# Seven-product second layer: halves of one expert's F instead of pairs of experts

## The chip, the cores and the metric

The kernel runs on one core of one Trainium2 chip. The metric is the time of one execution on the device, in microseconds (us). Engines are named as in the profile: PE (TensorE matmuls), PEld (its weight loads), DVE (VectorE), ACT (ScalarE), POOL (GpSimd), SP (SyncE, which issues most DMAs).

## The reference

Two stages, one after the other. The first is a gated linear attention over 4 sequences (batches) of 768 steps, 8 heads of 48: a state of 48 x 48 per head is decayed by a sigmoid gate, gets k v added, and is read with q. The second is a layer of four experts on the 3072 tokens of width 384:

```python
for t in range(S):
    state = f[:, :, t, :, None] * state + np.einsum('bhd,bhe->bhde', k[:, :, t], v[:, :, t])
    y[:, :, t] = np.einsum('bhd,bhde->bhe', q[:, :, t], state)
...
p = domain_probs / (domain_probs.sum(-1, keepdims=True) + 1e-09)
for e in range(E):                       # E = 4, w1[e]: 384 x 1024, w2[e]: 1024 x 384
    h = np.maximum(x @ w1[e], 0.0)
    out += p[:, e:e + 1] * (h @ w2[e])
```

All inputs and the output are float32; the kernel's matmuls work on bfloat16.

## The kernel before

**Work.** Time is cut into six chunks (c = 0 to 5) of 128 steps. One chunk has 4 x 128 = 512 tokens, four blocks of 128, one for each batch (b, or nt in the second layer). For each chunk the attention is computed first: loads of f, k, q, v; gates and their logarithms on ACT; cumulative sums on PE (`cs`, in chunk 0 also `cq`); exponentials; the products of q and k with them (`q c.b`, `k c.b`, line 385 or 388, on DVE or POOL); transposes (`tp`); scores (`at`), their masked eviction (`ev_at`); the output `y`; the state update. The result, transposed, is the input x of the expert layer.

**Expert layer.** The first product is h = relu(x w1[e]); F = 1024 is eight slices of 128 (`h c.e.fc.n0`, line 489, and `hs` for the later groups, line 521), evicted with relu on ACT or DVE. The second product is done in two ways.

- *Plain* (`mm_o`, line 504): chunk 0 (four blocks) and the first half of chunk 1 (two blocks), all four experts. For each block and expert eight matmuls with 384 moving columns, and one eviction of 128x384 that multiplies by the token's probability and adds to o (`ev_o`, line 511).
- *Seven products* (`mm_p`, line 558): from chunk 1's second half on, in groups of (chunk, half of the batches, pair of experts), named `c.hf.p`. The probabilities are put on y before, so that a pair of experts is one matrix product: rows are two blocks of 128 tokens, the inner side is the two experts of the pair, the output is two halves of 192 columns. Strassen's scheme in Winograd's form computes these 2 x 2 x 2 blocks with seven products instead of eight. It needs four sums of h blocks for each group (`s_sum`, line 539, 128x1024, on DVE, tiles S), and four differences of w2 blocks once for each pair (`t_sum`, line 548, 128x1536, on DVE; three go to `ts_sb`, the fourth replaces a part of w2 itself, so it must come after the pair's last plain product). Each product is eight matmuls of 192 columns into one PSUM bank; the bank is evicted into o (`ev_p`, line 566; 128x192), in the order 1, 2, 6, 5, 7, 3, 4. Banks X (1, 6, 7, 4) and Y (5, 3) go on accumulating after an eviction, so a later product of a bank waits for the eviction of the one before. The very last group, called TAIL (5.1.1), has the order 1, 2, 5, 6, 4, 7, 3 and stores some rows in halves.

**Order.** Everything is put into a list of `Op`s with a name, planned durations for the engines that can run it, a priority, dependences and buffers that it takes and frees ("rooms": 8 PSUM banks, 3 h, 6 S, 3 o tiles, and so on). `Plan.run` is a list scheduler: whenever an engine is free in the plan, it takes the ready step of lowest priority number. The instructions are then emitted in the planned order, and each engine's queue runs them in that order; what a step really waits for is a semaphore. `MOVES` is a string of named offsets on priorities, some with a fixed engine (`@DVE`). The priority of the expert layer is a counter, `unit`, that grows by one for each step of the layer. `zip_units` lays h of one expert beside the second product of the expert before; `zip_groups` does so for groups. DMA loads of the weights and of v are issued by POOL in the order `SEQ` (`v0 v1 v2 w0 v3 w1`, then the other pieces); the first two v wait for a k load to have landed (`GATE`). All other loads, the DMA transposes and the stores are issued by SP.

Of the kernel before, what the change touches and what calls it, by code (L numbers as in the profile page):

```python
# [9 lines left out]
BF16 = mybir.dt.bfloat16  # L10
# [5 lines left out]
    "ld f0.0=-58.8;ld f0.1=-61.7;ld k0.1=-53.8;ld f0.2=-42.3;ld k0.2=-2.1;ld v0.0=1520.4;w 0=-1521;ld v0.3=-2.1;w 5=-34.9;"  # L16
    "gate1 0.2=-7.8;cs 0.0=-2.4;expq 0.1=40.3;cs 0.1=-2.2;exps 0.1=-7;q 0.2=-0.1@DVE;ev_tp 0.3=196.8;ev_at0 0.0=17.1;ev_at1 0.0=13.1;"
    "ev_y 0.0=5.6;ev_at0 0.1=201.7;kv 0.0=-185.8;ld p=23.8;ev_tp 1.1=11.6@DVE;ev_y 1.1=-9.1;ev_ys 1.2.0.0=31.4@ACT;ev_ys 1.2.0.1=0@ACT;"
    "ld v2.2=16.8;h 0.0.4.0=27.1;h 0.0.4.128=38.5;h 0.0.4.256=24.1;o 0.2.0.1=1.7;h 0.3.2.0=11;h 0.3.4.0=12.2;h 0.3.6.0=-9.4;"
    "ev_o 0.2.3.0=-24;q 2.2=37;ev_at1 2.1=-11.4;xs 2.1.0=-40.5;ev_at0 2.2=26;xs 2.3.1=-2.9;ld f3.0=-13.6;ld q3.0=-1;ld f3.2=-3;"  # L20
    "ld v3.2=1.8;store 0.1.0=6.7;store 0.3.0=28.6;o 1.1.1.0=9;h 1.2.5.0=49.9;h 1.3.0.0=5.4;o 1.2.0.0=38.3;h 1.3.1.0=10;h 1.3.3.0=14.6;"
    "relu 1.3.6.0=7.5@ACT;t 1.1=-34;store 1.0.0=-1;o 1.3.1.0=-14.9;store 1.1.0=13.4;s2 1.1.0=-42.2;relu_s 1.1.1.0.0=5.1@DVE;"
    "ev_p 1.1.0.1=-44.4@DVE;p 1.1.0.2=-3.1;ev_p 1.1.0.2=-5.1;relu_s 1.1.1.0.2=5.9;p 1.1.0.6=7.9;p 1.1.0.5=3.9;ev_p 1.1.0.5=-49.4@DVE;"
    "relu_s 1.1.1.1.4=-0.1;relu_s 1.1.1.0.6=-2.9@DVE;egs 3.1=-4.1;v 3.1=4.7;tp 3.1=-27.9;tp 3.2=7.5;xs 3.1.0=-33.4;"
    "ev_ys 3.1.1.0=-36.5@DVE;ev_at0 3.3=-38.8;ev_kv 3.0=41.7;sf 3.0.3=21.3;kv 3.3=7.5;ld q4.0=-17.9;ld k4.2=18.2;ld q4.2=4.1;"
    "hs 2.0.0.1.2=-1.1;relu_s 2.0.0.1.4=67.6;hs 2.0.0.1.6=-7.8;hs 2.0.1.0.0=3;hs 2.0.1.1.2=-11.2;hs 2.0.1.1.4=-6.5;hs 2.0.1.1.6=3.3;"
    "hs 2.1.0.1.2=-6.2;ev_p 2.0.1.7=-10.7;hs 2.1.0.0.6=-11.8;hs 2.1.0.1.6=-7.5;s1 2.1.0=-35;p 2.1.0.1=3.8;p 2.1.0.2=22.9;"
# [110 lines left out]
def kernel(  # L138
# [11 lines left out]
    nc = tc.nc  # L150
# [27 lines left out]
    DH = Din // 2  # L178
    P = Plan(rooms)
# [48 lines left out]
    ts_sb = wpool.tile([128, NPR, 3, KF, DH], BF16)  # L228
# [273 lines left out]
    def mm_o(c, e, nt, fcs, part, cols):  # L502
        for fc in fcs:
            nc.tensor.matmul(out=tl("op", c, e, nt, part)[:, cols], lhsT=tl("h", c, e, half_of(c, nt * T))[:, fc, nt * T:(nt + 1) * T],  # L504
                             rhs=w2_sb[:, e, fc, cols], start=(fc == 0), stop=(fc == KF - 1))

    def ev_o(c, e, nt, part, cols, eng):
        op, o = tl("op", c, e, nt, part)[:, cols], tl("o", c, nt // 2)[:, nt % 2, cols]
        pe = pn[:, e, nt * C + c:nt * C + c + 1]
        if e > 0:  # L510
            nc.vector.scalar_tensor_tensor(out=o, in0=op, scalar=pe, in1=o, op0=ALU.mult, op1=ALU.add)
        elif eng == "ACT":
            nc.scalar.activation(out=o, in_=op, func=AF.Copy, scale=pe)
        else:
            nc.vector.tensor_single_scalar(out=o, in_=op, scalar=pe, op=ALU.mult)
# [15 lines left out]
    def block(c, hf, p, r, el):  # L531
        return tl("hs", c, hf, p)[:, el, :, r * T:(r + 1) * T]

    def s_sum(c, hf, p, j, fs):
        a = lambda r, el: block(c, hf, p, r, el)[:, fs]
        s = lambda i: tl("S", c, hf, p, i)[:, fs]
        in0, in1, op = {1: (lambda: (a(1, 0), a(1, 1), ALU.add)), 2: (lambda: (s(1), a(0, 0), ALU.subtract)),
                        3: (lambda: (a(0, 0), a(1, 0), ALU.subtract)), 4: (lambda: (a(0, 1), s(2), ALU.subtract))}[j]()
        return nc.vector.tensor_tensor(out=s(j), in0=in0, in1=in1, op=op)  # L539
# [3 lines left out]
    def t_sum(p, j):  # L543
        b = lambda el, cols: w2_sb[:, 2 * p + el, :, cols]
        t = lambda i: ts_sb[:, p, i - 1]
        o, in0, in1 = {1: (t(1), b(0, HI_), b(0, LO_)), 2: (t(2), b(1, HI_), t(1)), 4: (t(3), b(1, LO_), t(2)),
                       3: (b(0, HI_), b(1, HI_), b(0, HI_))}[j]
        return nc.vector.tensor_tensor(out=o, in0=in0, in1=in1, op=ALU.subtract)

    def mm_p(c, hf, p, m, bank, first):  # L550
        w = lambda el, cols: w2_sb[:, 2 * p + el, :, cols]
        lhs, rhs = {1: (lambda: block(c, hf, p, 0, 0), w(0, LO_)), 2: (lambda: block(c, hf, p, 0, 1), w(1, LO_)),
                    3: (lambda: tl("S", c, hf, p, 4), w(1, HI_)), 4: (lambda: block(c, hf, p, 1, 1), ts_sb[:, p, 2]),
                    5: (lambda: tl("S", c, hf, p, 1), ts_sb[:, p, 0]), 6: (lambda: tl("S", c, hf, p, 2), ts_sb[:, p, 1]),
                    7: (lambda: tl("S", c, hf, p, 3), w(0, HI_))}[m]
        lhs, out_ = lhs(), tl("mp", c, hf, p, bank)[:, 0:DH]
        for fc in range(KF):
            nc.tensor.matmul(out=out_, lhsT=lhs[:, fc, :], rhs=rhs[:, fc, :], start=(first and fc == 0), stop=(fc == KF - 1),  # L558
                             skip_group_check=True)
# [35 lines left out]
    wd = {}  # L595
    for j, x in enumerate(SEQ.split() + [f"w{i}" for i in range(SEQ.count("w"), len(pieces))]):
        i = int(x[1:])
        if x[0] == "v":
            issued.append(P.add(f"v issue {i}", {"POOL": 0.8}, lambda _, i=i: load(0, "v", i, 1), -600 + 2 * j,
                                deps=issued[-1:] + gate(x), takes=[("vb", 0, i)], lag=1.2))  # L600
            ld[0, "v", i] = P.add(f"ld v0.{i}", {"DMA": 1.1}, lambda _: None, VW[0] + j, deps=issued[-1:], lag=2.0)
# [9 lines left out]
        op = P.add(f"w {i}", {"DMA": 2.05 if i < 6 else 4.4}, lambda _: None, -400 if i == w_last else (VW[1] if i < 2 else -480) + j, deps=[iss], lag=1.0)  # L611
# [10 lines left out]
    def attention(c, slot, gran):  # L622
# [10 lines left out]
        for b in range(B):  # L633
# [18 lines left out]
            qm = P.add(f"q {c}.{b}", pe or ({"DVE": 0.85} if (c, b) < (1, 2) else {"POOL": 1.2}), one(product, 0), s(4) - 0.2,  # L652
                       deps=(eq or [ex]) + [ld[c, "q", b]], takes=[("qk", c, b)], frees=[("q", c, half), ("e", c, b)])
            km = P.add(f"k {c}.{b}", pe or ({"DVE": 0.545} if (c, b) < (1, 2) else {"POOL": 1.0}), one(product, 1), s(4) - 0.1,
# [97 lines left out]

    def add_o(c, e, nt, half):
        p = unit[0] + 0.5
        by_cols = (c, e, nt) == (C - 1, E - 1, B - 1)
        part = half if by_cols else 0
        cols = slice(half * Din // 2, (half + 1) * Din // 2) if by_cols else slice(0, Din)
        fcs = range(KF) if by_cols else range(half * 4, half * 4 + 4)
        key = ("ps_m", "op", c, e, nt, part)
        d = [hdone[k] for k in hdone if k[:2] == (c, e) and k[2] in fcs and k[3] <= nt * T]  # L760
        m = omm[c, e, nt] = P.add(f"o {c}.{e}.{nt}.{half}", {"PE": 0.645}, lambda _: mm_o(c, e, nt, fcs, part, cols), p,
                                  deps=d + (wd[e, 2] if by_cols or len(wd[e, 2]) == 1 else [wd[e, 2][half]]) + [omm.get((c, e, nt))], takes=[key], lag=0.2, frees=[("h", c, e, half_of(c, nt * T))])
        if half == 1 or by_cols:
            w = 0.36 if by_cols else 0.62
            ev = oev[c, e, nt] = P.add(f"ev_o {c}.{e}.{nt}.{part}", {"ACT": 0.58, "DVE": 0.56} if e == 0 else {"DVE": w},
                                       lambda g: ev_o(c, e, nt, part, cols, g), p - 1,
                                       deps=[m, oev.get((c, e - 1, nt)), pdone], takes=[("o", c, nt // 2)], frees=[key])
# [220 lines left out]
```

## Time and profile before

| | |
|---|---|
| time, median of 3 runs | 288.69 us (288.08 to 289.03) |
| span of the profiled execution | 284.9 us |
| median time less that span | 3.8 us |
| PE busy | 276.6 us (97%) |
| DVE, ACT, POOL busy | 195.9, 178.3, 111.2 us |
| plain second product (L504) | 192 matmuls of 384 columns |
| seven products (L558) | 1008 matmuls of 192 columns |
| first layer (L521, L489) | 864 and 264 matmuls |
| granted TensorE clock | 1.000 |

The profile is of one execution; the span is the time from its first to its last instruction. Its own time on the device's clock is not listed apart from the three runs, so the median stands for it: the last two lines of time differ by 3.8 us, which lie around the span. Busy time of PE overlaps, since matmuls are pipelined: a group's mean duration is a latency, and the distance from one start to the next has to be read from a run of matmuls. DMA transfers and queues appear in the chain of waits under the name of the engine that issues them (SPq is SP's queue).

### The profile page before, as it was taken

The numbers are of one execution on the slowest core, as the hardware profiler recorded it, in microseconds if no ns is written. First come the engines' busy times: TensorE is split into PE (matmuls) and PEld (weight loads), VectorE is DVE, ScalarE is ACT, GpSimd is POOL, SyncE is SP. The second block draws the span as 40 slices with busy tenths as digits, with TensorE's granted clock in tenths as the row PEclk, the third lists the DMA queues.
The fourth block names the chain that finished last, engine by engine and source line by source line (L and its number), as shares of the span: only waits on it lengthen the run. The fifth ranks groups of instructions, "written<-read, shape, count | busy, mean of one in ns | idle before, by whom it ended". The sixth has DMA issues, their size and how long they took to land.

```text
span 284.9 us, 7480 instructions
## 1 busy us (share of the span) xinstructions
PE 276.6 (97%) x3016; PEld 236.3 (83%) x3016; DVE 195.9 (69%) x394; ACT 178.3 (63%) x339; POOL 111.2 (39%) x183
## 2 busy tenths in 40 slices
PE   6789999999999999999999999999999999999994
PEld 3577555667777999999998999999999999999994
DVE  5893142797698897977888776887986876425543
ACT  6778546658777843873687755884576752555640
POOL 6599201236763834864039828164522000000000
PEclk9999999999999999999999999999999999999999
DMA  6999999988998999999989999898377241100101
GB/s 161 218 185 206 208 192 222 182 157 207 174 159 152 209 173 205 170 190 187 208 152 176 143 203 179 153 221 172 51 158 132 55 85 56 59 0 2 58 0 55
DMA packets 153686, 41.85 MB, mean 147 GB/s; under 512 B 144028, under 2 KB 152860, under 8 KB 153652
## 3 DMA queue, kind: packets, MB, share of 16 engines
q1 hardware_dynamic: 142404, 34.66, 62.9%
q0 software_dynamic: 11248, 6.72, 16.8%
q8 instruction: 23, 0.38, 0.6%
q14 instruction: 11, 0.09, 0.1%
HBM read 31.51 MB, written 4.72 MB: 127 GB/s over the span
## 4 chain that ended last, share of the span: by engine, by line
PE 93%; SPq 2%; DMA 2%; DVE 1%; ACT 1%; issue 0%; DVEq 0%
PE ps_m L521 33%; PE ps_m L558 29%; PE ps_m L504 11%; PE ps_m L489 11%; PE ps_m L428 2%; PE ps_m L455 2%; DMA q<-in_q_dram 2%; SPq L290 2%; PE ps_m L451 1%; PE ps_m L461 1%; PE ps_m L338 1%; SPq L292 1%; PE ps_m L397 0%; PE ps_m L480 0%; DVE AT L440 0%
## 5 line engine op out<-in xcount | busy, mean ns | idle before, releaser
L521 PE MATMUL ps_m<-x,w_sb 128*128 128x256 bf16 x864 | 107.8, 273 | 0.0
L529 ACT ACTIVATE h<-ps_m 128x512 bf16<-128x512 f32 x114 | 67.6, 597 | 63.4 <-PE ps_m L521 44.2
L521 PEld LDWEIGHTS <-w_sb 128*128 128x128 bf16 x864 | 82.7, 98 | 8.7
L558 PEld LDWEIGHTS <-S 128*128 128x128 bf16 x576 | 48.5, 98 | 1.4
L566 DVE TENSOR_TENSOR o<-ps_m,o 128x192 f32<-128x192 f32 x91 | 30.9, 351 | 23.1 <-PE ps_m L558 21.1
L558 PEld LDWEIGHTS <-h 128*128 128x128 bf16 x432 | 36.5, 98 | 0.8
L504 PE MATMUL ps_m<-w_sb,h 128*128 128x384 bf16 x192 | 36.0, 326 | 0.0
L489 PE MATMUL ps_m<-x,w_sb 128*128 128x128 bf16 (+2 forms) x264 | 35.8, 282 | 0.0
L476 POOL TENSOR_TENSOR Sf<-Sf,egs 48x192 f32<-48x192 f32 x40 | 21.3, 535 | 27.5 <-DVE Sf L468 15.4
L539 DVE TENSOR_TENSOR S<-h 128x1024 bf16<-128x1024 bf16 x36 | 25.6, 735 | 9.0 <-ACT h L529 8.9
L500 ACT ACTIVATE h<-ps_m 128x512 bf16<-128x512 f32 (+1 forms) x47 | 24.0, 519 | 11.8 <-PE ps_m L489 10.4
L444 DVE TENSOR_TENSOR AT<-ps_m,mask 128x512 bf16<-128x512 f32 x40 | 25.4, 682 | 5.3 <-PE ps_m L428 5.3
L504 PEld LDWEIGHTS <-h 128*128 128x128 bf16 x192 | 18.4, 98 | 12.4
L558 PE MATMUL ps_m<-ts_sb,S 128*128 128x192 bf16 x288 | 28.7, 246 | 0.0
L558 PE MATMUL ps_m<-w_sb,S 128*128 128x192 bf16 x288 | 28.5, 246 | 0.0
L558 PE MATMUL ps_m<-w_sb,h 128*128 128x192 bf16 x288 | 28.5, 246 | 0.0
L489 PEld LDWEIGHTS <-w_sb 128*128 128x128 bf16 x264 | 21.6, 98 | 8.3
L388 POOL TENSOR_TENSOR qk<-q,e 128x384 bf16<-128x384 f32 x18 | 21.7, 1214 | 14.9 <-DVE S L539 6.0
L527 DVE TENSOR_SCALAR h<-ps_m 128x512 bf16<-128x512 f32 x30 | 20.4, 690 | 10.2 <-PE ps_m L521 8.6
L371 ACT ACTIVATE e<-ps_m 128x384 f32<-128x384 f32 x40 | 23.3, 708 | 3.0 <-PE ps_m L338 2.2
L388 POOL TENSOR_TENSOR qk<-k,e 128x384 bf16<-128x384 f32 x18 | 19.2, 1073 | 12.5 <-PE ps_m L461 3.5
L411 ACT ACTIVATE yb<-ps_m,pn 128x384 bf16<-128x384 f32 x43 | 22.8, 581 | 1.3 <-PE ps_m L455 0.7
(87 smaller groups left out, 318.8 us busy)
## 6 DMA issues: line engine op xcount, KB each, us to landing
out_dram<-o SPq DMA_DIRECT2D x23, 192.0 KB, 2.5
w_sb<-in_moe_w_dram POOLq DMA_DIRECT2D x5, 768.0 KB, 14.5
k<-in_k_dram SPq DMA_DIRECT2D x10, 384.0 KB, 5.9
q<-in_q_dram SPq DMA_DIRECT2D x10, 384.0 KB, 5.1
v<-in_v_dram SPq DMA_DIRECT2D x10, 384.0 KB, 5.2
f<-in_f_logit_dram SPq DMA_DIRECT2D x9, 384.0 KB, 5.7
w_sb<-in_moe_w_dram POOLq DMA_DIRECT2D x6, 384.0 KB, 7.5
f<-in_f_logit_dram SPq DMA_DIRECT2D x6, 192.0 KB, 4.2
```

What stands on the lines that cost most here:

```text
L371: nc.scalar.activation(out=o, in_=i, func=AF.Exp, scale=1.0 if j else -1.0)
L388: return engines[eng].tensor_tensor(out=tl("qk", c, b)[:, j, :, 0:D].rearrange("t (i r) d -> t i r d", r=2), in0=tl("qk"[j], c, b // 2)[:, ...
L411: nc.scalar.activation(out=ys, in_=y, func=AF.Copy, scale=pe)
L444: nc.vector.tensor_tensor(out=tl("AT", c, b)[:, r].rearrange("s i t -> s (i t)"), in0=tl("A", c, b, r).rearrange("s i t -> s (i t)"), in1= ...
L489: nc.tensor.matmul(out=hp(c, e, fc, n0, n1, nf)[:, f], lhsT=w1_sb[:, e, kk, (fc + f) * 128:(fc + f + 1) * 128], rhs=tl("xT", c)[:, kk, n0: ...
L500: nc.scalar.activation(out=dst, in_=src, func=AF.Relu)
L504: nc.tensor.matmul(out=tl("op", c, e, nt, part)[:, cols], lhsT=tl("h", c, e, half_of(c, nt * T))[:, fc, nt * T:(nt + 1) * T], rhs=w2_sb[:, ...
L521: nc.tensor.matmul(out=out_[:, f], lhsT=w1_sb[:, e, kk, (fc + f) * 128:(fc + f + 1) * 128], rhs=tl("xs", c, hf, p)[:, el, kk, :], start=(k ...
L529: nc.scalar.activation(out=dst, in_=tl("hp", c, hf, p, el, fc), func=AF.Relu)
L539: return nc.vector.tensor_tensor(out=s(j), in0=in0, in1=in1, op=op)
L558: nc.tensor.matmul(out=out_, lhsT=lhs[:, fc, :], rhs=rhs[:, fc, :], start=(first and fc == 0), stop=(fc == KF - 1), skip_group_check=True)
L566: nc.vector.tensor_tensor(out=o, in0=src, in1=o, op=ALU.add)
```

## The change

1. The seven products of the later groups are cut otherwise. The inner side's two halves are now the two halves of one expert's F (`half_k`, four slices each) instead of the two experts of a pair. A group's product still sums over both experts of the pair (four matmuls each), into the same bank. S sums have the same size and count; their operands now have one more dimension.
2. The w2 differences (T) are made per expert: four experts x four of 128x768 instead of two pairs x four of 128x1536. Those of expert 1 come early (priority -100), those of the others late (60, and the one in place after the expert's last plain product).
3. One expert, `BLOCKED = (1,)`, uses seven products in chunk 0 and chunk 1's first half too (`add_s1`, `add_p1`, `mm_p1`, `ev_p1`). In chunk 0 one product covers both pairs of blocks (8 matmuls into one bank), in chunk 1's half one pair (4). Each product is evicted per pair of blocks as 128x192, with the probability as a factor.
4. The plan models the POOL-issued loads as one queue (`fifo`), lets chunk 1's first q and k products go to POOL as well, and takes the h tile of a group when its matmuls start (from the third on) instead of at their relu.
5. All offsets in `MOVES` are others. Among them: the order of chunk 0's loads, `k 0.3` to POOL, and large offsets on some products near the end (`p 4.0.0.5`, `p 4.1.1.7`, `p 5.0.1.3`, `p 5.1.0.5`, `p 5.1.1.5`), which the plan then takes only when nothing else is ready.

The branch of `add_o` for the last block by columns is removed; no block of the last chunk came to it before.

```diff
 MOVES = (
...
+    "ld f0.1=-2.5;ld k0.1=18.6;ld q0.1=21.5;ld f0.3=26.2;ld k0.2=20.5;ld q0.2=193.3;ld k0.3=25.9;ld q0.3=379.4;cq 0.0=85.3;"
+    "q 0.1=73.6@DVE;ev_tp 0.1=-55.3@DVE;cq 0.2=57.7;k 0.3=-19765.5@POOL;at 0.3=-88.9;xt 0.0=137.2;ld p=110.4;k 1.0=16.5@DVE;"
...
+    "p 3.1.1.1=-129.3;hs 4.0.0.0.4=54.9;p 3.1.1.7=38.1;hs 4.0.0.1.4=40.7;p 3.1.1.3=6.6;hs 4.0.1.0.0=69;p 4.0.0.5=405.8;"
...
+    "p 4.1.1.7=605;p 5.0.1.3=611.6;p 5.1.0.1=12.6;s2 5.1.1=38.7;p 5.1.0.5=155.8;ev_p 5.1.0.7=-31.5;p 5.1.1.5=534.2"
...
-    ts_sb = wpool.tile([128, NPR, 3, KF, DH], BF16)
+    ts_sb = wpool.tile([128, E, 3, KH, DH], BF16)
...
+    def block(c, hf, p, r, kh):
+        return tl("hs", c, hf, p)[:, :, half_k(kh), r * T:(r + 1) * T]
...
+    def t_sum(e, j):
+        b = lambda kh, cols: w2_sb[:, e, half_k(kh), cols]
+        t = lambda i: ts_sb[:, e, i - 1]
...
+    def factors(m, e, blk, s):
+        w = lambda kh, cols: w2_sb[:, e, half_k(kh), cols]
+        return {1: lambda: (blk(0, 0), w(0, LO_)), 2: lambda: (blk(0, 1), w(1, LO_)), 3: lambda: (s(4), w(1, HI_)),
+                4: lambda: (blk(1, 1), ts_sb[:, e, 2]), 5: lambda: (s(1), ts_sb[:, e, 0]), 6: lambda: (s(2), ts_sb[:, e, 1]),
+                7: lambda: (s(3), w(0, HI_))}[m]()
+
     def mm_p(c, hf, p, m, bank, first):
...
+        for el in range(2):
+            lhs, rhs = factors(m, 2 * p + el, lambda r, kh: block(c, hf, p, r, kh)[:, el],
+                               lambda i: tl("S", c, hf, p, i)[:, el * KH:(el + 1) * KH])
+            for f in range(KH):
+                nc.tensor.matmul(out=out_, lhsT=lhs[:, f, :], rhs=rhs[:, f, :], start=(first and el == 0 and f == 0),
+                                 stop=(el == 1 and f == KH - 1), skip_group_check=True)
+
+    def mm_p1(c, e, tps, m, bank, first):
+        for w in range(len(tps)):
+            out_ = tl("mp", c, "d", e, tps[0], bank)[:, w * DH:(w + 1) * DH]
...
+            for f in range(KH):
+                nc.tensor.matmul(out=out_, lhsT=lhs[:, f, :], rhs=rhs[:, f, :], start=(first and w == 0 and f == 0),
+                                 stop=(f == KH - 1), skip_group_check=True)
+
+    def ev_p1(c, e, tps, w, bank, r, cols, eng, new):
...
+        if not new:
+            nc.vector.scalar_tensor_tensor(out=o, in0=src, scalar=pe, in1=o, op0=ALU.mult, op1=ALU.add)
...
+    def add_s1(c, e, tps):
...
+            sum1[c, e, j] = P.add(f"s{j} {c}.d{e}", {"DVE": 0.72 if len(tps) == 2 else 0.45}, lambda _, j=j: s_sum1(c, e, tps, j), unit[0] - 2 + 0.1 * j,
+                                  deps=d + [sum1[c, e, before] if before else None], takes=[sk(j)], frees=[hk] + ([sk(before)] if before else []))
...
+        mm = P.add(f"p {c}.d{e}.{m}", {"PE": 0.33 * len(tps)}, lambda _: mm_p1(c, e, tps, m, bank, first), p, deps=d, takes=[key], lag=0.2,
+                   frees=[("S", c, "d", e, tps[0], s) if s else ("h", c, e, 0)])
...
     def ol(c, e, nts):
-        return [(c, e, nt, half) for nt in nts for half in range(2)]
+        if e in BLOCKED:
+            tps = sorted({nt // 2 for nt in nts})
+            return [lambda i=i: add_p1(c, e, tps, i) for i in range(7)]
+        return [lambda nt=nt, half=half: add_o(c, e, nt, half) for nt in nts for half in range(2)]
...
+    tdone, TP = {}, (60, -100)
...
+            tdone[e, j] = P.add(f"t {e}.{j}", {"DVE": 0.56}, lambda _, j=j: t_sum(e, j), unit[0] + e if late_ else TP[e in BLOCKED], deps=d)
...
-            km = P.add(f"k {c}.{b}", pe or ({"DVE": 0.545} if (c, b) < (1, 2) else {"POOL": 1.0}), one(product, 1), s(4) - 0.1,
+            km = P.add(f"k {c}.{b}", pe or ({"DVE": 0.555, "POOL": 1.0} if (c, b) < (1, 2) else {"POOL": 1.0}), one(product, 1), s(4) - 0.1,
...
+BLOCKED = (1,)
```

## The prediction

> **What bounds the kernel now.** I read the page's head first, then the busy time by stretches, then the waits of PE, then the groups with shapes kept apart, then the chain of waits, and last the timeline of the end.
>
> ```profile
> span 284.9 us, 7480 instructions
> PE 276.6 (97%) x3016; PEld 236.3 (83%) x3016; DVE 195.9 (69%) x394; ACT 178.3 (63%) x339; POOL 111.2 (39%) x183
> ```
>
> PE is busy 97% of the span. Where the other 3% lie decides what can be gained besides less work. The stretches (time, length, then busy us and instruction counts of PE, PEld, DVE, ACT, POOL):
>
> ```profile
> 10.00:15.00 5.00, 3.07 (x53) 2.12 (x49) 4.24 (x8) 3.28 (x9) 4.68 (x6) 1.00 1.66 205
> 20.00:25.00 5.00, 5.00 (x99) 5.00 (x97) 3.31 (x11) 4.29 (x8) 4.86 (x9) 1.00 1.27 207
> 60.00:80.00 20.00, 20.00 (x179) 14.76 (x177) 15.88 (x31) 14.38 (x30) 13.70 (x20) 1.00 0.95 178
> 80.00:100.00 20.00, 20.00 (x229) 16.64 (x227) 17.11 (x35) 16.47 (x31) 12.16 (x23) 1.00 0.86 168
> 280.00:285.00 5.00, 1.31 (x16) 1.08 (x14) 1.37 (x5) 0.00 (x0) 0.00 (x0) 1.00 0.16 59
> ```
>
> From 20 us to 280 us PE is never idle. The only waits of PE are these, 4.5 us together, and the timeline puts each before 18 us:
>
> ```profile
> PE ps_m L940 <- DVE S L185: 1.5, 1, 1.5
> PE ps_m L428 <- DVE QK L279: 1.3, 2, 1.0
> PE ps_m L342 <- ACT gp L330: 0.8, 1, 0.8
> PE ps_m L353 <- ACT gp L330: 0.5, 1, 0.5
> PE ps_m L397 <- ACT QK L278: 0.4, 1, 0.4
> ```
>
> Busy could still hide slow spacing, so I took matmul starts from the trace: after 19 us no start is more than 0.1 us later than its neighbour's own length allows. So the time is three terms: a start of 19.1 us, a PE stream of 262.2 us without holes (to 281.3), and a drain of 3.6 us. The stream can only be shortened by fewer columns; everything else in it can only open holes. The timed median, 288.69, is 3.8 us above the span; I take that as unchanged and count all differences against the span.
>
> **Products: the term that is removed.** Expert 1 of chunk 0 (four token blocks) and of chunk 1's first half (two) loses (4+2) x 8 = 48 matmuls of 384 columns (L504). It gains 7 products x 4 matmuls of 192 columns per pair of blocks: three pairs, 84 matmuls, the form of L558. A group's mean is a latency (326 and 246 ns) and overlaps its neighbours, so spacing is read from the chain:
>
> ```profile
> 29.04 3.90 PE ps_m L504 x24
> 274.05 7.28 PE ps_m L558 x88
> ```
>
> 3.90/24 = 162.5 ns and 7.28/88 = 82.7 ns. Removed 48 x 162.5 = 7.80 us, added 84 x 82.7 = 6.95 us: **-0.85 us** of PE, all on the path, since nothing else fills PE. A short matmul needs its weights sooner:
>
> ```profile
> L558 PEld LDWEIGHTS <-S 128*128 128x128 bf16 x576 | 48.5, 98 | 1.4
> L511 DVE SCALAR_TENSOR_TENSOR o<-ps_m,pn,o 128x384 f32<-128x384 f32 x18 | 10.8, 613 | 8.4 <-PE ps_m L504 5.9 <-ACT h L500 2.5
> L566 DVE TENSOR_TENSOR o<-ps_m,o 128x192 f32<-128x192 f32 x91 | 30.9, 351 | 23.1 <-PE ps_m L558 21.1
> L539 DVE TENSOR_TENSOR S<-h 128x1024 bf16<-128x1024 bf16 x36 | 25.6, 735 | 9.0 <-ACT h L529 8.9
> L548 DVE TENSOR_TENSOR ts_sb<-w_sb,ts_sb 128x1536 bf16<-128x1536 bf16 x4 | 4.4, 1106 | 7.1 <-DMA w_sb<-in_moe_w_dram 7.1
> ```
>
> A load takes 98 ns, more than 82.7, and still 88 matmuls in a row kept 82.7: loads overlap. If they did not, 84 x 98 = 8.23 us, +0.43 instead of -0.85. The later groups keep their 56 matmuls; only the halves that meet change. I cost that at 0.
>
> **DVE work that this adds.** Short rows are estimated on the line through S (128x1024, 678 ns at the shortest) and T (128x1536, 948): 0.53 ns per column, so 0.54 us for a T of 768 columns and 0.41 for an S of 512. In chunk 0: four S of 1024 columns (4 x 0.735 = 2.9) and 14 evictions of 192 columns for 4 of 384 (14 x 0.351 - 4 x 0.613 = 2.5). Expert 1's four T (2.2 us) stand where three T of the first pair stood (28 to 41 us, 2.9). DVE is busy 14.1 of the 35 us from 25 to 60, so 5 us fit. The first T that needs expert 1's w2 waited 7.1 us for its load and ran at 36.4; products need these sums, but the stream at 36 to 41 us has h of expert 2 (24 matmuls x 216 ns = 5.2 us) to cover four T. Cost 0; if that cover were used up, four T, 2.2 us. In chunk 1 (60 to 100 us): four short S (1.6), seven evictions for two (7 x 0.351 - 2 x 0.612 = 1.2), and up to 12 short T for the 5 that lie there (6.5 - 5.3 = 1.2): +4.0 us on 33.0 of 40. DVE keeps 3.0 us idle there where it had 7.0. It is not the bound as an average, so I take 0; the bounds are 0 and one late chain of four S, 1.6 us, more if several are late. Products of chunk 1 may go to POOL (1.07 to 1.21 us each against 0.55 to 0.85 on DVE), which has 14 of 40 us free there. The S of later groups keep count and size, reading two runs of 4x128: 0, bounds -0.05 to +0.02 us each (678 to 751 against 735), off the path.
>
> **The start.** By the priorities the loads now leave SP as f0 f1 k0 q0 f2 k1 q1 k2 f3 k3, probabilities, q2, q3; before, k1 f2 stood ahead of k0, and the probabilities last. The gate on v0 moves from the third load to the sixth. The first h could not start before w1's first piece, whose landing records end at 18.85 us (its weights load at 19.0). Loads and v queue on busy DMA engines from 3 us on, and the bytes ahead of that piece are the same, so this end stays: 0. One of batch 3's products goes to POOL (1.36 us there by the plan, 1.07 by the nearest row) ahead of w's issues; issues run about 6 us ahead of landing, which hides it. q2 landed at 12.4 and q3 at 14.0 (the trace); one and two places later is +1.6 and +0.7 us. h of batches 0 and 1 (24 matmuls x 56 ns = 1.3 us) and w's second piece cover most of that. Bounds -0.3 to +1.0, taken 0.
>
> **The end.** The last three products now end, as the priorities read, with product 3 of the last pair instead of 7, and products from earlier groups (3 of 5.0.1, 7 of 4.1.1, 5 of 4.0.0) are held back to fill PE.
>
> ```profile
> 280.69 0.36 DVE L566 TENSOR_TENSOR o<-ps_m,o 128x192 f32<-128x192 f32 x1 [0.30 <-PE ps_m L558]
> 281.35 0.62 DVE L566 TENSOR_TENSOR o<-ps_m,o 128x192 f32<-128x192 f32 x2 [0.30 <-PE ps_m L558]
> ```
>
> Before, two evictions follow the last matmul, then a store of a whole row (issue 282.17, landed 283.99, 1.8 us; half rows took 1.6). One eviction and half a row save 0.3 + 0.2; but 3 must wait for 5's eviction (0.36 plus about 0.2 of signals), which costs 0.5 where no held product covers it, and a held product that ends last stores a whole row. Bounds -0.5 to +0.5, taken **-0.2**.
>
> Sum: 284.9 - 0.85 - 0.2 = 283.85; with 3.8 around it 287.65, say **287.6**.
>
> **The rivals.** (A) The stream stays dense: 287.6, from 287.1 to 288.1. For: no hole in 262 us before, three engines with room. (B) Holes in chunk 1's first half: S sums and evictions queue behind T on DVE, PE waits for them. For: 3.0 us of idle left in 40, one T already took 1.57 us against 0.95. Against: PE has h matmuls to run ahead with. One S chain late at the products (1.6) plus one T ahead of it in the queue (0.5): 287.6 + 2.1 = 289.7; it decides from 1.3 us of holes on, where the gain is gone, and a second chain gives 291.3. The Trainium skill (GPSIMD Engine Reference, 1. Specifications) says that GpSimd shares its SBUF interfaces with VectorE, with contention for DVE instructions that have two SBUF inputs, as S and T have; the 1.57 us row agrees with it, without proving that cause. (C) The start slips by 0.5 to 1.0 us as q2 and q3 come late: 288.3, no change that can be told. (D) Weight loads bound the short products, the change doesn't do what it says: 287.6 + 0.85 + 0.43 = 288.9. Against: the 88 matmuls above. The Trainium skill (TensorE: Matmul & The Clock Gate, LDWEIGHTS) gives a load as its columns over 1.2 GHz, 107 ns here, which taken as spacing would make the products 9.0 us, 1.2 us slower than before; the trace's 98 ns and 82.7 ns stand against it.
>
> **How the numbers follow.** A 0.53, B 0.26, C 0.19, D 0.02. A change under 0.3% (0.87 us) is about what a measurement of this kernel can't tell from none. A is faster by more than that up to 287.8: 0.45 of its 0.53, the rest same. B is slower in 0.24 and same in 0.02. C is same in 0.17 and slower in 0.02; D is same. Together faster 0.45, same 0.29, slower 0.26. The range reaches from A's lower end with 0.2 of start, 286.9, to B with some more holes, 290.2: below it about 0.05, above 0.1. A's own range is 287.1 to 288.1.
>
> **What would show it.** In the changed profile: PE busy down 0.8 to 0.9 us; L504's count 144 and 84 more of 192 columns at 83 ns; no wait of PE after 20 us; first h at 19 us; one eviction after the last matmul. It is wrong if PE waits for DVE's S, T or evictions between 30 and 100 us, if the first dense stretch starts later than 20 us, or if the last store is issued over 1 us after the last matmul.

## The result, and the profile after

The changed kernel takes 290.08 us (median of 7 executions, 288.33 to 292.57), the kernel before 288.08 us beside it (7 executions, 287.16 to 289.03). The ratio is 1.008, 95% interval 1.0053 to 1.0107: slower by 2.0 us. The forecast was 287.6 and faster; the time lies in the range, near its upper end, but none of the rivals named what happened.

The head of the page and the counts of the groups first:

```profile
span 288.8 us, 7586 instructions
PE 279.3 (97%) x3050; PEld 241.8 (84%) x3055; DVE 205.1 (71%) x422; ACT 179.5 (62%) x338; POOL 111.9 (39%) x187
```

```profile
L513 PE MATMUL ps_m<-w_sb,h 128*128 128x384 bf16 x144 | 26.0, 326 | 1.6 <-DMA w_sb<-in_moe_w_dram 1.5
```

The products were replaced as read: 144 plain matmuls where 192 stood (L513 is L504 of before). The new ones keep the spacing that the prediction took, as two runs of matmuls in the chain of waits show (L597 is expert 1's products):

```profile
75.36 2.60 PE ps_m L513 x16
77.96 0.66 PE ps_m L597 x8
```

2.60/16 = 162.5 ns and 0.66/8 = 82.5 ns, so 48 plain matmuls less and 84 short ones more are -0.87 us of PE work. The wait at the end of the L513 row is the first thing the prediction didn't have. The span is 3.9 us longer than in the profile before (284.9), and this execution's own time is 290.47, 1.7 us above its span. Now PE's waits, and busy time by stretches (columns as before: stretch, length, busy us and counts of PE, PEld, DVE, ACT, POOL, then granted clock, DMA share, GB/s):

```profile
PE ps_m L513 <- DMA w_sb<-in_moe_w_dram: 1.5, 1, 1.5
...
PE ps_m L406 <- DVE qk L394: 0.9, 1, 0.9
PE ps_m L498 <- DMA w_sb<-in_moe_w_dram: 0.3, 1, 0.3
```

```profile
17.00:20.00 3.00, 2.66 (x27) 2.17 (x25) 1.97 (x6) 1.78 (x4) 2.97 (x5) 0.52 0.98 75
20.00:24.00 4.00, 4.00 (x48) 3.61 (x47) 2.74 (x5) 1.55 (x3) 3.93 (x8) 0.50 1.09 160
...
60.00:100.00 40.00, 38.46 (x417) 30.27 (x416) 32.31 (x70) 27.49 (x54) 24.03 (x37) 1.00 0.93 184
```

Three readings. From 17 to 24 us PE ran at half the granted clock (0.52, 0.50; in the profile before it was 1.00 throughout): nearly 7 us of which half is lost, 3.4 us. The DMA engines moved 75 GB/s from 17 to 20 us (14 from 18 to 19, where it was 208 before) and 160 after; in 20 to 25 us they moved 151 where they had moved 207. And PE lost 1.54 us in 60 to 100 us, in one piece at 60.8, waiting for w2 of expert 3. The two heads give the same sum: PE is busy 2.7 us longer (the lost clock less the products) and idle 1.2 us longer, 3.9 us together. The first h is not later (18.86 us, 19.09 before). DVE, where rival B looked, is busy 32.31 us of 60 to 100 (32.99 before), and PE has no hole of over 0.1 us after 63 us.

So the transfers of the weights are late. POOL issues them; its timeline, after and then before (start, duration, engine, line, operation; in brackets the idle time before it and what ended it):

```profile
12.00 1.02 POOL L397 TENSOR_TENSOR qk<-k,e 128x384 bf16<-128x384 f32 x1
12.95 0.80 POOL L312 DMA_DIRECT2D w_sb<-in_moe_w_dram  x1
13.75 0.92 POOL L293 DMA_DIRECT2D vb<-in_v_dram  x1
14.67 0.65 POOL L441 TENSOR_SCALAR_AFFINE_SELECT AT<-AT 128x512 bf16<-128x512 bf16 x1
16.53 1.00 POOL L397 TENSOR_TENSOR qk<-k,e 128x384 bf16<-128x384 f32 x1 [1.21 <-ACT yb L287]
17.48 0.80 POOL L312 DMA_DIRECT2D w_sb<-in_moe_w_dram  x1
```

```profile
12.06 0.76 POOL L303 DMA_DIRECT2D w_sb<-in_moe_w_dram  x1
12.79 0.93 POOL L284 DMA_DIRECT2D vb<-in_v_dram  x1
13.71 0.75 POOL L303 DMA_DIRECT2D w_sb<-in_moe_w_dram  x1
14.45 1.19 POOL L432 TENSOR_SCALAR_AFFINE_SELECT AT<-AT 128x512 bf16<-128x512 bf16 x1
15.60 1.55 POOL L303 DMA_DIRECT2D w_sb<-in_moe_w_dram  x2
```

Two products of k (batches 2 and 3 of chunk 0), not one, now run on POOL, each ahead of a weight issue. The second stands behind the mask of batch 1, and then POOL is idle for 1.21 us. The profile names a step of ACT there, which ended at 15.87; what ended last is on DVE. The kernel makes a product on POOL wait for the product that DVE has ahead of it in the plan (`turn`), here q of batch 3, which ended at 16.39:

```profile
15.85 0.54 DVE L394 TENSOR_TENSOR qk<-q,e 128x384 bf16<-128x384 f32 x1
```

While POOL waits, every issue behind the product waits too. The second weight issue goes out at 17.48 where it went at 13.71, 3.8 us later, and all later ones follow.

| weight piece | 0 | 1 | 2 | 3 | 4 | 6 | 9 | 10 |
|---|---|---|---|---|---|---|---|---|
| landed, before (us) | 18.68 | 20.54 | 22.50 | 24.40 | 26.74 | 32.03 | 45.26 | 56.75 |
| landed, after (us) | 18.81 | 22.33 | 25.48 | 27.79 | 30.15 | 35.75 | 49.70 | 62.28 |

(Last landing record of each piece, from the span's start as in the timelines; the prediction's 18.85 is this 18.68.) The first product costs piece 0 only 0.13 us. From piece 1 on the delay grows, from 1.8 us to 3.4 by piece 4 and 5.5 by piece 10. Piece 10 is issued only when chunk 1's first k load has landed (47.50 before, 51.84 after), which stands behind these transfers.

The end went nearly as foretold: one eviction after the last matmul.

```profile
284.54 0.82 PE L589 MATMUL ps_m<-ts_sb,h 128*128 128x192 bf16 x8
285.40 0.36 DVE L616 TENSOR_TENSOR o<-ps_m,o 128x192 f32<-128x192 f32 x1 [0.30 <-PE ps_m L589]
```

### The profile page after: what moved, and what is told of

Read it like the earlier page. It is cut to its first block, busy times and chain, and to the rows that moved or that the text cites. A ratio compares the mean times of both kernels' runs of the same rounds, so it can differ in the third digit from the quotient of the medians.

```text
span 288.8 us, 7586 instructions
## 1 busy us (share of the span) xinstructions
PE 279.3 (97%) x3050; PEld 241.8 (84%) x3055; DVE 205.1 (71%) x422; ACT 179.5 (62%) x338; POOL 111.9 (39%) x187
## 4 chain that ended last, share of the span: by engine, by line
PE 77%; DMA 14%; POOL 3%; SPq 3%; issue 1%; DVE 0%; ACT 0%; POOLq 0%; DVEq 0%
PE ps_m L530 33%; PE ps_m L589 29%; DMA w_sb<-in_moe_w_dram 10%; PE ps_m L513 5%; PE ps_m L498 4%; DMA k<-in_k_dram 3%; POOL w_sb L312 2%; PE ps_m L437 2%; SPq L299 2%; PE ps_m L464 1%; DMA q<-in_q_dram 1%; PE ps_m L460 1%; SPq L301 1%; PE ps_m L347 1%; PE ps_m L470 1%; PE ps_m L597 1%
## 5 line engine op out<-in xcount | busy, mean ns | idle before, releaser
L530 PE MATMUL ps_m<-x,w_sb 128*128 128x256 bf16 x864 | 104.8, 273 | 0.0
L530 PEld LDWEIGHTS <-w_sb 128*128 128x128 bf16 x864 | 82.8, 98 | 9.5
L616 DVE TENSOR_TENSOR o<-ps_m,o 128x192 f32<-128x192 f32 x91 | 31.6, 354 | 26.3 <-PE ps_m L589 23.6
L498 PE MATMUL ps_m<-x,w_sb 128*128 128x128 bf16 (+2 forms) x260 | 37.0, 292 | 0.6 <-DMA w_sb<-in_moe_w_dram 0.3
L589 PEld LDWEIGHTS <-h 128*128 128x128 bf16 x432 | 36.5, 98 | 0.6
L397 POOL TENSOR_TENSOR qk<-q,e 128x384 bf16<-128x384 f32 x19 | 22.5, 1197 | 26.9 <-ACT o L287 11.0
L509 ACT ACTIVATE h<-ps_m 128x512 bf16<-128x512 f32 (+1 forms) x42 | 22.0, 526 | 15.7 <-PE ps_m L498 12.5
L498 PEld LDWEIGHTS <-w_sb 128*128 128x128 bf16 x264 | 23.1, 104 | 8.5 <-DMA w_sb<-in_moe_w_dram 0.6
L513 PE MATMUL ps_m<-w_sb,h 128*128 128x384 bf16 x144 | 26.0, 326 | 1.6 <-DMA w_sb<-in_moe_w_dram 1.5
L420 ACT ACTIVATE yb<-ps_m,pn 128x384 bf16<-128x384 f32 x46 | 24.3, 584 | 3.6 <-PE ps_m L464 2.7
L287 ACT COPY o<-ps_m 128x192 f32<-128x192 f32 x34 | 10.8, 319 | 20.5 <-PE ps_m L589 19.6
```

The lines of the kernel that those rows point to most:

```text
L397: return engines[eng].tensor_tensor(out=tl("qk", c, b)[:, j, :, 0:D].rearrange("t (i r) d -> t i r d", r=2), in0=tl("qk"[j], c, b // 2)[:, ...
L420: nc.scalar.activation(out=ys, in_=y, func=AF.Copy, scale=pe)
L498: nc.tensor.matmul(out=hp(c, e, fc, n0, n1, nf)[:, f], lhsT=w1_sb[:, e, kk, (fc + f) * 128:(fc + f + 1) * 128], rhs=tl("xT", c)[:, kk, n0: ...
L509: nc.scalar.activation(out=dst, in_=src, func=AF.Relu)
L513: nc.tensor.matmul(out=tl("op", c, e, nt)[:, 0:Din], lhsT=tl("h", c, e, half_of(c, nt * T))[:, fc, nt * T:(nt + 1) * T], rhs=w2_sb[:, e, f ...
L530: nc.tensor.matmul(out=out_[:, f], lhsT=w1_sb[:, e, kk, (fc + f) * 128:(fc + f + 1) * 128], rhs=tl("xs", c, hf, p)[:, el, kk, :], start=(k ...
```

## The experiments

Theory 1: POOL's two k products delay the weight issues, the DMA queue runs dry, and PE's lost time follows from late weights. Rivals: the half clock alone is the loss; or the new products or offsets are worse further on. Unless it says otherwise, an edit reorders or reassigns steps of the planned list `done` just before emission, and leaves the rest of the plan as it was.

**E1: both k products back on DVE.**

```diff
+    for o in done:
+        if o.name in ("k 0.2", "k 0.3"):
+            o.engine = "DVE"
```

> The changed kernel with k 0.2 and k 0.3 given back to DVE at the same place of the plan, so that POOL issues the weights w0, w1, w2 without those two products ahead of them; nothing else differs. Theory 1 (late weights: the two products on POOL delay the issues, the load queue runs dry around 20 us, each later piece of weights lands 2 to 5 us later and PE waits for the last one at 60.7 us): w1 issued near 15 us instead of 17.7, last piece landed by 58 to 59 us instead of 62.4, no wait of PE on weights, time 287.0 to 288.0. Theory 2 (PE's half clock from 17 to 24 us alone costs the 3.5 us): 290 within 0.7, unless the clock stays at 1.000 in this run. Theory 3 (the added sums and evictions on DVE): 290 within 0.5.

288.56 us (10 executions, 286.99 to 290.32) beside 287.78: ratio 1.0019 (0.9992 to 1.0047). Most of the loss is gone, not all of it: the time is above Theory 1's 287.0 to 288.0. Issue 1 now goes out at 14.78 and lands at 21.10, but issue 2 still goes at 17.65, behind the mask of batch 2, which itself waits 1.54 us for ACT, and 2 to 10 land 0.5 to 2.9 us later than in the kernel before. PE's waits on weights, which Theory 1 had gone, show what is left:

```profile
PE ps_m L513 <- DMA w_sb<-in_moe_w_dram: 1.2, 1, 1.2
...
PE ps_m L498 <- DMA w_sb<-in_moe_w_dram: 0.7, 1, 0.7
```

**E2: the kernel before, with its two k products on POOL** and issue 1, a mask and issue 2 moved behind the second.

```diff
+    for o in done:
+        if o.name in ("k 0.2", "k 0.3"):
+            o.engine = "POOL"
+    held = [o for o in done if o.name in ("w issue 1", "mask1 0.1", "w issue 2")]
+    done = [o for o in done if o not in held]
+    at = [o.name for o in done].index("k 0.3") + 1
+    done[at:at] = held
```

> The kernel before with only k 0.2 and k 0.3 moved to POOL, and POOL's w issue 1, mask1 0.1 and w issue 2 emitted behind k 0.3, as the changed kernel has them; no product and no offset is changed. Theory 1: weights land 2 to 5 us later and the kernel before gets slower by 1.5 to 4 us (289.5 to 292). Theories 2 and 3: within 0.5 of the kernel before (288.1), except for what the clock takes if it falls here too.

290.67 us (4 executions, 290.55 to 293.82), ratio 1.0129 (1.0068 to 1.019). The size fits, the reason doesn't: its largest wait is on the mask that I had moved along, not on weights.

```profile
PE ps_m L455 <- POOL AT L432: 2.4, 2, 1.2
```

It shows that a POOL queue that stands in front of PE costs over 1%, but can't tell late weights from a late mask.

**E3: the changed kernel with nine dummy matmuls of 512 columns in PE's holes from 13 to 19 us**, to hold the clock.

```diff
+    for o in done:
+        o.pad += {"tpq 0.2": 3, "y 0.1": 1, "tpq 0.3": 1, "kv 0.1": 1, "xt 0.1": 1, "h 0.0.0.0": 2}.get(o.name, 0)
```

> The changed kernel with nine more dummy matmuls of 512 columns on PE between 13 and 19 us, in gaps that PE has there, to keep its clock up. Theory 1: the clock is 1.000, but time stays at 290.0 within 0.7, and the wait for the last weights at 61 us grows by what the clock gives back (1.7 to 4 or 5 us). Theory 2: 286.5 to 287.5. Theory 3: 290 or less by what the clock gives.

289.34 us (10 executions, 288.53 to 291.32), ratio 1.0066 (1.0039 to 1.0094). The clock was 0.998 or more in every execution, and still the kernel is slower: what full clock gives, PE spends waiting.

```profile
PE ps_m L513 <- DMA w_sb<-in_moe_w_dram: 1.6, 1, 1.6
...
PE ps_m L498 <- DMA w_sb<-in_moe_w_dram: 0.9, 1, 0.9
```

The holes lie at 21.3 (0.9 us), 28.9 (1.6) and 61.1 (0.1), 2.6 us in all; Theory 1 had the wait at 61 us grow instead. So the half clock of the first profile is no cause by itself: at half clock PE reaches late weights late, at full clock it waits for them.

**E4: the changed kernel without the gate of the last weight piece** on chunk 1's first k load.

```diff
-        if i == w_last:
-            after(ins["w", i], ins[1, "k", 0])
```

> The changed kernel without the wait that holds the last piece of weights (w2 of expert 3) back until chunk 1's first k load has landed; POOL then issues it near 35 us. Theory 1: the wait of PE for it at 61 us goes; time down by 1 to 2 us (288 to 289), unless chunk 1's loads, which now come some 4 us later, are the next to be late. Theories 2 and 3: 290 within 0.5.

290.81 us (4 executions, 290.38 to 291.41), ratio 1.0109 (1.0072 to 1.0146). Piece 10 lands at 53.88 instead of 62.28 and the wait at 60.8 is gone, but chunk 1's own loads (k at 55.37 instead of 51.84) pay for it:

```profile
PE ps_m L345 <- ACT gp L340: 1.9, 1, 1.9
PE ps_m L496 <- DMA w_sb<-in_moe_w_dram: 1.8, 1, 1.8
```

The first wait (at 53.3 us) is on chunk 1's gates, the second (at 20.6 us) on piece 1. This edit moved the delay and didn't remove it.

**E5: E1, and the weight issues 1 to 5 moved ahead of POOL's masks and state steps.**

```diff
+    for o in done:
+        if o.name in ("k 0.2", "k 0.3"):
+            o.engine = "DVE"
+    for name, ahead_of in (("w issue 1", "mask1 0.1"), ("w issue 2", "mask1 0.2"), ("w issue 3", "mask1 0.2"), ("w issue 4", "sf 0.0.0"), ("w issue 5", "sf 0.0.1")):
+        o = next(o for o in done if o.name == name)
+        done.remove(o)
+        done.insert([x.name for x in done].index(ahead_of), o)
```

> The changed kernel with k 0.2 and k 0.3 on DVE and, besides, POOL's issues of w1 to w5 emitted ahead of the masks and state steps that stood in front of them, in the order of the kernel before; the plan is otherwise that of the changed kernel. Theory 1 (late weights): the first six pieces land as in the kernel before (w2 by 23, w4 by 27 us), PE no longer waits for weights between 20 and 62 us, and time is 286.7 to 287.5, 0.3 to 1.1 below the kernel before on this chip (287.8) for the 0.85 us of removed PE work. Rival (the added sums, evictions or the new order itself cost time): it stays at the 288.6 of the kernel with the two products on DVE alone.

286.73 us (12 executions, 285.72 to 287.69) beside 288.46: ratio 0.9941 (0.9922 to 0.996). It beats both kernels, and by more than the 0.85 us of removed work. Part of that is the clock: 8 of these 12 executions stand at 0.997 or more, and 6 of the 23 of the kernel before beside them. The rate from 15 to 20 us is 188 GB/s (116 in the changed kernel, 184 before), pieces 1 to 4 land within 0.8 us of the kernel before, and PE is dense from 60 to 100 us with the same products and the same offsets:

```profile
15.00:20.00 5.00, 3.86 (x70) 3.09 (x71) 4.41 (x11) 2.57 (x5) 4.57 (x8) 1.00 1.44 188
...
60.00:100.00 40.00, 40.00 (x423) 32.01 (x421) 32.41 (x72) 30.18 (x59) 25.91 (x41) 1.00 0.90 180
```

One part of Theory 1 failed: PE still waits for weights once before 62 us, at 58.3, for piece 10, which landed at 59.50.

```profile
PE ps_m L513 <- DMA w_sb<-in_moe_w_dram: 1.2, 1, 1.2
```

The profile is of the longest of the twelve executions (span 286.0, where the median at that clock is 284.7), so most of them may not have this wait.

**E6: a pair on the products alone.** Both kernels have the changed code with the offsets (`MOVES`) of before; the second also leaves expert 1 plain in chunk 0 and chunk 1's first half:

```diff
-BLOCKED = (1,)
+BLOCKED = ()
```

> The changed code, seven products for expert 1 included, with all offsets of the kernel before (MOVES). Theory 1: the old offsets keep the early issue of weights, so the product change alone gives at most its 0.85 us back where the plan stays dense: 287 to 289. Rival (the product change itself costs time on DVE): over 289, with PE waiting for S, T or evictions.

> The same with BLOCKED = (), so no expert uses seven products in chunk 0 and chunk 1's first half: the changed code and the old offsets without the product change. Theory 1: within 0.5 of the kernel before (287.8), or up to 0.9 above its sister with the products. Rival (products cost time): faster than its sister.

293.34 us (4 executions, 293.21 to 293.95) and 294.05 (4, 293.71 to 294.19), ratios 1.0182 (1.0146 to 1.0217) and 1.0197 (1.0167 to 1.0228). The pair's difference, -0.7 us, has the sign and about the size of the products' term, but it doesn't show it: the intervals overlap, the two have different plans, and the plain one has more half clock (0.988 in three of its four executions, where the other has 0.994 in three). They are 4.9 and 5.6 us above the kernel before, where 287 to 289 was expected of the first: with the old offsets the plan of the new code is worse (small holes of PE from 57 to 162 us), with or without the products. What the other offsets are worth by themselves can't be read from this.

**E7: the kernel before, with weight issues 1, 2 and 3 moved behind the mask of batch 2**, no product moved.

```diff
+    held = [o for o in done if o.name in ("w issue 1", "w issue 2", "w issue 3")]
+    done = [o for o in done if o not in held]
+    at = [o.name for o in done].index("mask1 0.2") + 1
+    done[at:at] = held
```

> The kernel before with only POOL's issues of w1, w2 and w3 emitted behind mask1 0.2, about 4 us later (w1 at 17.8 us instead of 13.9); no product, no offset, no engine is changed. Theory 1: w1 to w10 land 2 to 4 us later, PE waits for weights, time 289.3 to 290.5. Rival (late weights are covered, and the loss came from something else): 287.8 within 0.5.

288.98 us (10 executions, 288.06 to 290.79), ratio 1.0025 (1.0001 to 1.0049): slower by 0.5 us than the 288.46 beside it, less than Theory 1 gave and no more than its rival allows. Issue 1 went out at 17.30, near the changed kernel's 17.48, piece 1 landed at 22.29 (22.33 there), and the rate fell to 50 GB/s from 17 to 20 us. Pieces 2 and 3 came at 24.21 and 26.43, over a us earlier than there (25.48 and 27.79), because their issues follow at once (18.05, 18.82) instead of behind further POOL work. Pieces 4 to 10 landed 2.3 to 2.7 us later than in the kernel before, where the changed kernel has 3.4 to 5.5, and in this profile PE waited for none of them. So weights that are late by some 2.5 us cost little here; at which delay the full price sets in is not shown.

**E9: the changed kernel with weight issues 0 to 5 moved ahead, the k products left on POOL.**

```diff
+    for name, ahead_of in (("w issue 0", "k 0.2"), ("w issue 1", "mask1 0.1"), ("w issue 2", "mask1 0.1"), ("w issue 3", "k 0.3"), ("w issue 4", "mask1 0.2"), ("w issue 5", "sf 0.0.0")):
+        o = next(o for o in done if o.name == name)
+        done.remove(o)
+        done.insert([x.name for x in done].index(ahead_of), o)
```

> The changed kernel with both k products left on POOL, but with the weight issues 0 to 5 ahead of them (w 0 ahead of k 0.2, w 1 and w 2 ahead of the mask of batch 1 and of k 0.3, w 3 ahead of the mask of batch 2). It parts the two halves of the run that was faster than both kernels. Theory 1 (the late issues of the weights alone make the loss): w 1 is issued at about 13.7 us and lands by 21.4, the clock stays at 0.95 or more in 15 to 25 us, span 286 to 286.5 and time 287 to 287.8. Rival (the k products themselves come too late on POOL, 1.0 us each against 0.55 on DVE and behind POOL's other work, so that PE has too little before 20 us whatever the weights do): w 1 early all the same, but the clock in 15 to 25 us stays under 0.9 or PE waits for scores of batch 2 and 3; time 288.5 to 289.5.

288.11 us (12 executions, 286.67 to 289.06) beside 287.91: ratio 1.0007 (0.9985 to 1.0028). The median lies between the two forecasts, and each side is half right. In its profile (span 285.0, clock 0.998, the fastest of the twelve) weights are early (piece 1 at 21.09) and no wait on `w_sb` is left, as Theory 1 has it, but PE waits for POOL, as the rival has it:

```profile
PE ps_m L406 <- POOL qk L397: 0.8, 1, 0.8
PE ps_m L464 <- POOL AT L441: 0.7, 1, 0.7
```

In 10 of the 12 executions the mean clock was lower than in this one (0.986 to 0.994), with spans of 285.2 to 287.3. That opened a second question: does the clock by itself move this kernel?

**E8: the kernel before once more.**

> The kernel before, once more, for a second profile of it. My sum stood against a span of 284.9 and put 3.8 us around it. If what lies around the span is 1.7 us, as in all other kernels profiled, and the first profile was a quick execution, this span is 285.2 to 287.7 and its own time 1.7 us above it. If 3.8 us belongs to the kernel before, time less span is 3.8 us here.

288.79 us with a span of 287.1: 1.7 us around it, as everywhere. And this profile of the very same kernel has the half clock:

```profile
10.00:15.00 5.00, 2.52 (x40) 1.72 (x37) 3.81 (x8) 3.19 (x8) 4.12 (x5) 1.00 1.50 192
15.00:20.00 5.00, 4.99 (x66) 4.41 (x68) 4.14 (x10) 3.08 (x7) 4.97 (x8) 0.50 1.36 173
20.00:25.00 5.00, 5.00 (x85) 4.80 (x81) 2.81 (x7) 3.46 (x7) 4.86 (x9) 0.82 1.25 204
```

PE was idle half of 10 to 15 us, in holes of at most 1.1 us, and then ran at 0.50 from 15 us on. In the first profile of this kernel it was busy 3.07 of the 5 us, and the clock stayed. The landings differ as well: piece 1 at 21.96 and piece 10 at 58.50, 1.4 and 1.8 us later than in the first profile. Two executions of one kernel can differ by that much, so of the changed kernel's delays those of 3.4 us and more carry the argument, and not the 1.8 us of piece 1.

**E10 and E11: holes filled.** E10 is the kernel before with six dummy matmuls of 512 columns, E11 is E9 with four.

```diff
+    for o in done:
+        o.pad += {"cq 0.3": 3, "at 0.2": 3}.get(o.name, 0)      # E10
+        o.pad += {"y 0.1": 2, "tpk 0.3": 2}.get(o.name, 0)      # E11
```

> The kernel before with six dummy matmuls of 512 columns in two of PE's holes (three ahead of cq 0.3 near 12 us, three ahead of at 0.2 near 14 us). Its executions differ: span 285.45 us in the median where the mean granted clock is 0.997 or more, 286.15 at 0.991 to 0.996, 287.1 below 0.991. Theory 2 (PE's holes at 12 to 15 us set the clock granted after them, and that sets the span): with the holes filled nearly all executions stand at 0.997 or more, spans about 285.5, median time 287.1 to 287.4, 0.5 to 0.8 us below the kernel before, ratio 0.997 to 0.998. Rival (clock and span both follow something else, such as later loads, and a filled hole turns into a wait as in the changed kernel with fillers): median 287.9, ratio 1.000 to 1.003, waits of PE for w_sb of 0.5 us or more.

> The changed kernel with weight issues 0 to 5 ahead of the k products, which stay on POOL, now with four dummy matmuls of 512 columns (two ahead of y 0.1 near 16 us, two ahead of tpk 0.3 near 17.7 us). Without them its median was 288.11 us at a mean clock of 0.991, but its two executions at 0.998 had spans of 285.0 and 285.2. Theory 2 (early weights cure the waits; the k products on POOL leave PE holes at 16 to 18 us, and only the clock after these keeps it from the gain): clock 0.997 or more, spans about 285.1, median 286.7 to 287.2, ratio 0.995 to 0.998. Rival (the holes are the k products' own cost, and clock only goes with it): median 287.8 to 288.5, with waits of PE where the half clock was.

E10: 287.19 us (12 executions, 286.79 to 288.72) beside 287.97, ratio 0.9979 (0.996 to 0.9997), the clock at 0.997 or more in all twelve, where the kernel before has it in 13 of 42 on the same chip: Theory 2, in size too (a 0.4 us wait on `w_sb` appeared in its profile). E11: 287.23 us (12, 286.66 to 288.48), ratio 0.998 (0.996 to 1.0); the clock held in 7 of 12 only, so these four fillers are not enough to hold it.

With that, executions can be compared at like clock. Each has a span and a mean granted clock; medians of the span, with the count of executions (those of the kernel before are pooled from the runs beside E1 to E11, so the rows come from more than one chip):

| | clock under 0.991 | 0.991 to 0.996 | 0.997 and over |
|---|---|---|---|
| before | 287.1 (23) | 286.2 (37) | 285.45 (22) |
| after | 288.8 (1) | 290.9 (1) | 288.2 (5) |
| E1, k products on DVE | | 287.1 (6) | 286.45 (4) |
| E3, after with fillers | | | 287.6 (10) |
| E5, E1 and early issues | | 285.3 (4) | 284.7 (8) |
| E9, early issues alone | 286.75 (6) | 285.9 (4) | 285.1 (2) |
| E10, before with fillers | | | 285.5 (12) |
| E11, E9 with fillers | 286.7 (2) | 286.1 (3) | 285.2 (7) |

The columns are steps: in the clock records of the profiles the half clock before the last matmul comes in stretches of 3.41 us, and none, one or two of them give 0.997 and over, 0.994 and 0.988. Five of after's seven executions had the full clock, and were 2.75 us longer than the kernel before at that clock, so the half clock is not what they lost.

The chips differ too: the last entry of the kernel before is 284.9 (3), 286.0 (6) and 285.4 (13) on the three chips of E1 to E11. Beside the kernel before on their own chip and in the last column, E3 is 2.2 us longer, E1 1.05, E9 0.2, while E11 is 0.2 shorter and E5 1.3 (0.9 in the middle column). The chip of after's executions is not listed, but its ratio has a kernel before beside it. By the ratios the changed kernel is at +0.8%, E1 at +0.2%, E9 at +0.1% and E5 at -0.6%: the k products on DVE give back about 1.8 us, early issues alone about 2.1, both together about 4.

## Why the prediction was wrong

**The step that failed** is "The start", the k product on POOL: "issues run about 6 us ahead of landing, which hides it". An issue does run over 6 us ahead (12.06 to a last landing at 18.68), and for the one product ahead of the first issue that was enough: piece 0 landed 0.13 us later. But piece 0 had that cover from the transfers that were already issued, and the later pieces lost it when the issues stopped: POOL made none after the one at 13.75 us until 17.48, and the rate fell to 75 GB/s from 17 to 20 us. From 25 to 60 us the rate was no higher than before (about 196 GB/s against 202), and the delay stayed.

The price of one POOL instruction ahead of an issue was its duration at most (1.0 us) only if nothing else came in; here 1.21 us of waiting for DVE, the place behind the mask, and a second product that I missed added to it. I read the one offset in `MOVES` that names POOL, for k of batch 3. The plan chose POOL for k of batch 2 by itself, as the code of both kernels allows in chunk 0 (`pe = {"DVE": 0.47, "POOL": 1.36}`). The planned list, which the code makes before anything runs, has both products on POOL and the end of `w issue 1` at 18.1 us where it was 14.5, so the delay could have been read there.

Taken 0, bounds -0.3 to +1.0; in the runs 3.5 to 4 us (288.2 against E5's 284.7 at full clock, or 1.008 against 0.9941 of the kernel before). About half of it goes with the products (E1), the other half with the order of issues among POOL's masks and state steps, which I didn't cost at all. That late weights are the main link, and not the products' own lateness, is shown by E9, which leaves both on POOL and wins most of the loss back, and by the waits of E3; E9's waits of 0.8 and 0.7 us for POOL are what the products and masks add there. E7 shows that a shorter delay costs far less than I would have put on it.

**"No wait of PE after 20 us"** failed with it: 1.54 us at 60.8. The chain is piece 10's gate on a load that stands behind the delayed pieces (E4 moved the wait and didn't remove it).

**The range: luck.** 290.08 lies inside 286.9 to 290.2, but the upper end was set by rival B's holes on DVE, which did not come. And the forecast of 287.6 has two slips that go against each other, a short span and too much time around it (see the base below).

**Products, -0.85: right** as PE work: 84 matmuls at 82.5 ns for 48 at 162.5 are -0.87 us. How much of it reaches the time depends on the rest: at full clock and on one chip E5 is 1.3 us shorter than the kernel before, and E11 0.3 shorter than E10 with k products still on POOL.

**DVE, 0: right.** DVE's busy time rose by 9.2 us, most of it before 60 us (21.83 of 25 to 60 us against 14.14, more than the 5 us I had made room for), and not from 60 to 100, where I had put +4.0 (32.31 against 32.99). PE waited for none of the sums or evictions. Rival B did not occur, nor D. Rival C (the start slips) had nearly the right place and the wrong cause: q of batch 2 did come late (PE waited 0.9 us for its product at 13.9 us), but the first h started at 18.86 us (19.09 before), and the time was lost behind it.

**The end, -0.2: right.** From the last matmul's start to the end of the span it is 3.65 us against 3.85. One eviction follows, as foretold, but of product 4 of group 4.1.1, a held one, and not product 3 of the last pair.

**The base.** I put 3.8 us around the span by setting a median beside one profile. It is 1.7 to 1.9 us in every execution that lists both; the profile was of a short execution (284.9; the kernel before has 285.45 at the best clock in the median, 287.1 at the worst). With 1.7 instead of 3.8 the same sum gives some 285.5. The differences against the span were not harmed, but a stretch "1.00" from one profile was read as a property of the kernel, while most executions of the kernel before lose 0.7 to 1.7 us to the clock.

What stays open: what each of the changed offsets is worth, which of them make 5 us of difference in E6, and why E7's delay costs so little.

## What to carry to other kernels

An in-order engine that issues DMAs is a transfer resource: before putting compute on it, list what each issue will stand behind, with that compute's own waits, and ask whether the DMA queue has work until the next issue. If the code plans its own order, compare the planned times of the issues in both kernels. Here the transfers that started late stayed late to the last piece, so the price showed 40 us further on, as a wait, and curing the wait moved it (E4). When the expected gain of a kernel is under 1%, compare executions at like granted clock and on the same chip, and don't take the clock of one profile for the kernel's.

## What the runs showed of the hardware

The granted TensorE clock fell to half without any long idle time of PE. The clock records give stretches at 0.50 of 3.41 us (E2, E6 at 91 us, E7, E11) or 6.82 us (the changed kernel, E8, the plain kernel of E6). The longest hole of PE in the 3.41 us ahead of the drop was 1.03 us in E8, where PE was busy 1.36 of the 3.41 us, and 0.9 us in the changed kernel, where it was busy 2.52. How busy PE was doesn't decide it alone: E4 kept its clock through 3.41 us with only 1.77 busy (18.81 to 22.22) and most of a hole of 1.76 us in it. The same kernel lost the clock in some executions and not in others, and three dummy matmuls in each of two holes prevented it in 12 of 12 (E10). What exactly sets it stays open.

The Trainium skill (TensorE: Matmul & The Clock Gate, What's actually happening) says that the gate has two states, full and half, and watches a free-running window of about 3.4 us, so that the phase differs from run to run; the values, the lengths and the spread agree. Its table of the two states gives the half state as coming after an idle window, and there the traces differ: PE was never idle for 3.4 us ahead of a drop here.
